# Queries loaded as pairs of tokens, and turned by products with the identity into every other column

## The chip, the cores and the metric

The kernel runs on one NeuronCore of a Trainium2 chip. The core has five engines with instruction streams of their own: TensorE (PE, matrix products; its weight loads are listed apart as PEld), VectorE (DVE), ScalarE (ACT), GpSimd (POOL) and SyncE (SP), which here only issues DMAs. Sixteen DMA engines carry all transfers. SBUF is the on-chip memory of 128 partitions; PSUM takes the results of TensorE. The metric is the device time of one execution in microseconds (us).

## The reference

Linear attention with decay (4 batches, 8 heads, 768 tokens, head dimension 64), and a mixture of 8 experts behind it, of which each token takes 2. Cut to what matters:

```python
for b in range(nb):                                    # blocks of 64 tokens
    qb, kb, vb = (q[:, :, sl], k[:, :, sl], v[:, :, sl])
    intra = np.einsum('bhic,bhjc->bhij', qb, kb) * Dmask[None]
    intra = np.einsum('bhij,bhjd->bhid', intra, vb)
    inter = np.einsum('bhid,bhde->bhie', qb * lam_pow[None], kv_state)
    out[:, :, sl] = intra + inter
    kv_state = lam_block[None, :, None, None] * kv_state + np.einsum('bhsd,bhse->bhde', kb_dec, vb)
x = out.transpose(0, 2, 1, 3).reshape(3072, 512)
# gate: logits and noise scale from x, the two best of 8 experts for each token, their softmax weights
for e in range(8):
    out2[mask] += top2_w[mask, k, None] * (np.maximum(x[mask] @ w1[e], 0.0) @ w2[e])
```

q, k and v are float32 in HBM, laid out (batch, head, token, 64): the 64 numbers of one token and one head are 256 bytes in a row, and the next token of the same head follows them directly.

## The kernel before

The attention takes the first 140 us or so, the experts the rest. The attention works in chunks of C = 128 tokens, two chunks (a = 0 and 1) to a step, and u = 0 to 11 numbers the 12 steps (NST); three steps make a batch (NW). Heads are taken in pairs (HP = 4 pairs), so that a pair's 2 x 64 numbers fill 128 partitions.

`load(u, nm)` brings a step's k, q or v to SBUF, tokens on the partitions: two transfers on SP's queue, one for each chunk, each 128 tokens x 8 heads x 64 numbers. `trans_k(u)` and `trans_q(u)` turn keys and queries, so that the 64 numbers of a head lie on the partitions and the tokens along them: for each chunk four transposes of 128 x 128 on TensorE, one for each pair of heads, into a bank of PSUM, which ACT (DVE at u = 0) copies to SBUF; for the queries DVE makes beside it qTs, the copy multiplied by the decay QS. `scores(u)` multiplies turned queries and keys, and DVE multiplies the mask in (tile `at`). `kv(u)` makes the state, `intra` and `inter` the two parts of the output (PSUM banks pO and pKV), `kdecay` the decayed keys (ACT), `evac_o` brings the output to SBUF (ACT, tile xo), `products` and `logits` multiply it with the gate's weights, `turn_x` and `store_x` bring it to the tensor x_tok in HBM (one DMA of 512 KB on SP).

The order of the work is that of the program: each engine executes its own instructions in the order in which the loop writes them. The pass t of the loop turns keys and queries of u = t + 1, issues the loads of step t + 3, and does the second half of step t; it also issues the first expert's weights (`load_w`, tile wst, 512 KB each, on SP, at the end of the passes t = 2, 4, 5, 6, 7, 8, 10, 11), and ACT and POOL split them one pass later (`split_high`, `split_low`: tiles w1h, w2h and w1l, w2l):

```python
for t in range(NST):
    u = t + 1
    if t: products(t - 1); turn_x(t - 1)
    trans_k(u);  load(t + 3, "kt")
    trans_q(u);  load(t + 3, "qt")
    kv(u);       kdecay(t + 2)
    intra(t);    load(t + 3, "vt")
    if t: store_x(t - 1)
    inter(t, 0); evac_o(t);  logits(t - 1)
    scores(u);   inter(u, 1)
    ...
```

At the end of a pass stand routing work of earlier steps, the splitting of weights and `load_w`. The tiles kt and qt have two buffers and vt has three; PSUM has four banks under the name pS, which transposes, kv and scores use in turn. SP's DMAs signal by eight semaphores in turn, and an issue waits for the DMA that used its semaphore before, so at most eight of them are under way. In the order listings such a wait reads DMAHW0_49 to DMAHW7_49, and other waits name the engine.

At the very start two small transfers on ACT's queue make the mask: powd<-pwt (L196, to HBM) and at<-powd (L211, back in another order), then Mk (L203, L204), with which DVE's first `at` products (L361) empty the banks that kv(0) needs.

Of the kernel before, what the change touches and what calls it, by code (L numbers as in the profile page):

```python
# [26 lines left out]
AF = mybir.ActivationFunctionType  # L27
# [3 lines left out]
B, H, S, D = 4, 8, 768, 64  # L31
C = 128
NC = S // C
NCH = B * NC
HP = H // 2
# [20 lines left out]
NW = NC // 2  # L56
# [31 lines left out]
def sub(ap, offset, dims):  # L88
    return bass.AP(tensor=ap.tensor, offset=ap.offset + offset, ap=dims)
# [27 lines left out]
def kernel(  # L117
# [3 lines left out]
    nc = tc.nc  # L121
# [20 lines left out]
    QT, KT, VT = {}, {}, {}  # L142

    def load(u, nm):

        if u >= NST:
            return
        b, w = divmod(u, NW)
        at = b * H * S * D + w * 2 * C * D
        store, src, n = {"qt": (QT, q, 2), "kt": (KT, k, 2), "vt": (VT, v, 3)}[nm]  # L150
        store[u] = aw.tile([128, 2, H, D], FT, name=nm, bufs=n)
        for a in range(2):
            nc.sync.dma_start(store[u][:, a], sub(src, at + a * C * D, [[D, 128], [S * D, H], [1, D]]))  # L153

# [17 lines left out]
    for nm in ("kt", "qt"):  # L172
        load(0, nm)
    jp = ac.tile([128, 128], I32, name="jp")
    nc.gpsimd.iota(jp, pattern=[[1, 128]], base=0, channel_multiplier=-1)
    identf = consts.tile([128, 128], FT, name="identf")
# [16 lines left out]
    p = psum.tile([128, H], FT, name="pL")  # L193
    nc.tensor.transpose(p, pw[:, 1:129], identf[:H, :H])
    nc.scalar.activation(pwt[:, 0, :], p, AF.Copy)
    nc.scalar.dma_start(powd.rearrange("(a m) h -> m a h", a=2), pwt)  # L196
    mrev = aw.tile([128, C, H], FT, name="at")
    load(0, "vt")
    Mk = [ac.tile([128, HP, C], FT, name=f"Mk{s}") for s in range(2)]
    kdc = pwt[:, 0, :, None]  # L200
# [5 lines left out]
    QS = ac.tile([128, HP, C], FT, name="QS")  # L206
    p = psum.tile([128, HP, C], FT, name="pL")
# [12 lines left out]
    for nm in ("kt", "qt", "vt"):  # L220
        load(1, nm)
# [77 lines left out]
    qT, qTs, kT, KD, AT, XO, XP, PO, SA, first = {}, {}, {}, {}, {}, {}, {}, {}, {}, {}  # L299
# [3 lines left out]
    def bank():  # L303
        return psum.tile([128, HP, C], FT, name="pS", bufs=4)

    def half(i):
        return slice(i * 64, (i + 1) * 64)
# [13 lines left out]
    def trans_q(u, scaled=True):  # L321

        qT[u] = aw.tile([128, HP, 2 * C], FT, name="qT", bufs=1)
        qTs[u] = aw.tile([128, HP, 2 * C], FT, name="qTs")
        for a in range(2):
            p = bank()
            for hp in range(HP):
                nc.tensor.transpose(p[:, hp, :], QT[u][:, a, 2 * hp:2 * hp + 2, :], identf)  # L328
            cs = slice(a * C, (a + 1) * C)
            if u:  # L330
                nc.scalar.activation(qT[u][:, :, cs], p, AF.Copy)
            else:
                nc.vector.tensor_copy(qT[u][:, :, cs], p)
            if scaled and (u % NW or a):
                nc.vector.tensor_mul(qTs[u][:, :, cs], p, QS)

    def kdecay(u):
        if u >= NST:
# [297 lines left out]
    load_wgn(6)  # L636
    trans_k(0)
    trans_q(0, False)
    nc.vector.tensor_mul(qTs[0][:, :, C:], qT[0][:, :, C:], QS)
    make_mask()  # L640
# [297 lines left out]
    for t in range(NST):  # L938
        u = t + 1
# [7 lines left out]
        if u < NST:  # L947
            trans_q(u)
# [49 lines left out]
    hp = ctx.enter_context(tc.tile_pool(name="hp", bufs=1, reuse_waits="tile"))  # L998
# [189 lines left out]
    with tc.For_i(0, n_over) as it:  # L1188
# [3 lines left out]
        rows = lst[bass.ds(row, OV), :]  # L1192
# [12 lines left out]
        for f in range(FB):  # L1205
            p = psum.tile([128, OV], FT, name="pS", bufs=4)
            for d in range(DB):
                for i, (a, b) in enumerate(((0, 0), (0, 1), (1, 0))):
                    nc.tensor.matmul(p, W1[a][d][:, f * 128:(f + 1) * 128], xt(b, slice(0, OV))[:, d],
                                     start=(d == 0 and i == 0), stop=(d == DB - 1 and i == 2))  # L1210
# [3 lines left out]
        p = psum.tile([OV, DM], FT, name="pO")  # L1214
        for f in range(FB):
            for i, (a, b) in enumerate(((0, 0), (0, 1), (1, 0))):
                nc.tensor.matmul(p, ht(0, a, f, slice(0, OV)), W2[b][f // 2][:, f % 2, :],
                                 start=(f == 0 and i == 0), stop=(f == FB - 1 and i == 2))
# [31 lines left out]
```

## Time and profile before

| | |
|---|---|
| median of 3 runs | 731.28 us (727.81 to 733.37) |
| the profiled execution | 724.91 us |
| its span, first to last instruction | 723.1 us |
| PE busy | 700.6 us, 97% |
| DVE, ACT, POOL busy | 358.2, 237.6, 282.8 us |
| mean granted clock of TensorE | 0.995 |
| moved by DMA | 122.50 MB, 138698 packets, of them 87658 under 512 bytes |

A row of the profile gives a line of the code, an engine, an operation and "out<-in". One product of the code in float32 stands as two matmuls in the trace, a transpose as one. The chain of waits follows, backward from the last instruction, what each piece of work waited for; in order of time its columns are start, length and what it was. "Idle" of an engine is put down to what released it.

### The profile page before, as it was taken

How to read it: one execution, taken by the hardware profiler on the slowest of the kernel's cores; microseconds unless marked ns; L12 is line 12 of the kernel's file. 1: busy time of each engine (PE TensorE's matmuls, PEld its weight loads, DVE VectorE, ACT ScalarE, POOL GpSimd, SP SyncE). 2: the span in 40 equal slices, each digit the busy share in tenths (PEclk: the TensorE clock that was granted, in tenths of full speed). 3: DMA queues.
4: the chain of work that ended last, by engine and by line, in shares of the span. 5: the costliest groups of instructions: out<-in, count | busy, mean ns of one | idle time of the engine just before them, and what ended most of it. 6: DMA issues, size and time to landing. Idle time of an engine off the chain costs nothing.

```text
span 723.1 us, 13507 instructions
## 1 busy us (share of the span) xinstructions
PE 700.6 (97%) x4910; PEld 598.6 (83%) x4910; DVE 358.2 (50%) x815; ACT 237.6 (33%) x451; POOL 282.8 (39%) x446
## 2 busy tenths in 40 slices
PE   7999998799998999999999999999999999999996
PEld 5888887698897898898889888888888898889885
DVE  6345969777325564564445344534353454335211
ACT  1667776331123422142313231323231331314100
POOL 5210446677846453623262325124322423221311
PEclk9999999999999999999999999999999999999998
DMA  9999997971508567656456645656465656540211
GB/s 199 206 242 232 238 256 206 294 226 39 118 13 282 180 168 208 212 167 187 131 203 170 183 148 180 190 166 211 135 187 160 205 174 180 160 144 19 76 44 39
DMA packets 138698, 122.50 MB, mean 169 GB/s; under 512 B 87658, under 2 KB 106474, under 8 KB 138628
## 3 DMA queue, kind: packets, MB, share of 16 engines
q1 hardware_dynamic: 124852, 84.69, 44.2%
q0 software_dynamic: 13360, 36.38, 16.2%
q8 instruction: 40, 0.66, 0.4%
q10 hardware_dynamic: 416, 0.53, 0.3%
q14 instruction: 30, 0.25, 0.1%
HBM read 87.15 MB, written 35.55 MB: 170 GB/s over the span
## 4 chain that ended last, share of the span: by engine, by line
PE 81%; issue 6%; DMA 4%; SPq 3%; POOL 2%; ACT 1%; DVE 1%; another core or an unknown queue 1%; POOLq 0%; ACTq 0%
PE pS L861 36%; PE pO L899 15%; PE pKV L899 14%; SPq L153 2%; PE pS L358 2%; PE pKV L371 2%; DMA wst<-in_moe_w_dram 2%; PE pO L371 2%; PE pO L904 2%; PE pS L328 1%; PE pS L431 1%; PE pKV L904 1%; PE pS L315 1%; POOL out_dram L918 1%
## 5 line engine op out<-in xcount | busy, mean ns | idle before, releaser
L861 PE MATMUL pS<-xtl,w1h 128*128 128x512 f32 (+3 forms) x544 | 180.7, 332 | 1.4 <-DVE xtl L826 0.9
L861 PE MATMUL pS<-xth,w1h 128*128 128x512 f32 (+3 forms) x544 | 181.0, 333 | 0.4 <-ACT xth L825 0.4
L861 PE MATMUL pS<-xth,w1l 128*128 128x512 f32 (+3 forms) x544 | 180.4, 332 | 0.0
L867 ACT ACTIVATE ht<-pS 128x512 fp32r<-128x512 f32 (+3 forms) x136 | 65.3, 483 | 220.6 <-PE pS L861 146.1
L871 DVE SCALAR_TENSOR_TENSOR ht<-pS,ht 128x256 fp32r<-128x256 f32 (+3 forms) x176 | 76.2, 453 | 111.8 <-ACT ht L867 98.9
L899 PE MATMUL pKV<-w2h,ht 128*128 128x512 f32 x384 | 123.0, 391 | 0.0
L899 PE MATMUL pO<-w2h,ht 128*128 128x512 f32 x384 | 122.7, 391 | 0.0
L861 PEld LDWEIGHTS pS<-xtl,w1h 128*128 128x128 f32 x544 | 102.8, 189 | 10.7 <-DVE xtl L826 1.2
L861 PEld LDWEIGHTS pS<-xth,w1h 128*128 128x128 f32 x544 | 102.7, 189 | 9.7 <-ACT xth L825 0.5
L918 POOL DMA_INDIRECT out_dram<-ot,rec x46 | 61.6, 1340 | 124.9 <-DVE ot L911 112.7
L861 PEld LDWEIGHTS pS<-xth,w1l 128*128 128x128 f32 x544 | 102.8, 189 | 8.7
L899 PEld LDWEIGHTS pKV<-w2h,ht 128*128 128x128 f32 x384 | 72.1, 188 | 16.2
L899 PEld LDWEIGHTS pO<-w2h,ht 128*128 128x128 f32 x384 | 72.1, 188 | 16.1
L899 PE MATMUL pKV<-w2l,ht 128*128 128x512 f32 x192 | 75.5, 393 | 0.0
L899 PE MATMUL pO<-w2l,ht 128*128 128x512 f32 x192 | 75.4, 393 | 0.0
L814 POOL DMA_INDIRECT xg<-x_tok,rec x46 | 49.7, 1080 | 58.6 <-DMA rec<-lst 42.5
L883 POOL DMA_INDIRECT pv<-out_dram,rec x46 | 47.0, 1022 | 28.2 <-issue 28.2
L624 POOL DMA_INDIRECT lst<-recs,dest x48 | 48.3, 1007 | 11.8 <-issue 10.5
L1164 POOL COPY spacer<-ht 1x1 f32<-1x1 f32 x53 | 9.4, 177 | 106.7 <-ACT ht L867 106.6
L911 DVE SCALAR_TENSOR_TENSOR ot<-pKV,rec,pv 128x512 f32<-128x512 f32 x21 | 15.8, 751 | 66.8 <-PE pKV L899 56.9
L911 DVE SCALAR_TENSOR_TENSOR ot<-pO,rec,pv 128x512 f32<-128x512 f32 x21 | 15.7, 750 | 61.5 <-PE pO L899 59.3
L847 ACT ACTIVATE xth<-xg 128x512 fp32r<-128x512 f32 (+1 forms) x39 | 22.4, 598 | 69.0 <-DMA xg<-turned 69.0
(229 smaller groups left out, 944.8 us busy)
## 6 DMA issues: line engine op xcount, KB each, us to landing
wst<-in_moe_w_dram SPq DMA_DIRECT2D x48, 512.0 KB
turned<-ot SPq DMA_DIRECT2D x36, 256.0 KB
xg<-turned SPq DMA_DIRECT2D x144, 64.0 KB
wst<-in_moe_w_dram SPq DMA_DIRECT2D x32, 256.0 KB
kt<-in_k_dram SPq DMA_DIRECT2D x24, 256.0 KB
qt<-in_q_dram SPq DMA_DIRECT2D x24, 256.0 KB
vt<-in_v_dram SPq DMA_DIRECT2D x24, 256.0 KB
x_tok<-xc SPq DMA_DIRECT2D x12, 512.0 KB
```

The lines of the kernel that those rows point to most:

```text
L371: nc.tensor.matmul(PO[u][a][half(g), hp, :], lhs, rhs, start=n == 1, stop=n == (8 if u % NW or a else 4))
L624: st = nc.gpsimd.indirect_dma_start(out=lst, out_offset=bass.IndirectOffsetOnAxis(ap=r["dest"][:, i, c:c + 1], axis=0), in_=r["rec"][:, c, ...
L814: nc.gpsimd.indirect_dma_start(out=XG[t][:size(e, t)], out_offset=None, in_=x_tok[:rows, :], in_offset=bass.IndirectOffsetOnAxis(ap=at, ax ...
L847: nc.scalar.activation(hi, p, AF.Copy)
L861: nc.tensor.matmul(p, W1[a][d][:, fs], xt(b, cs)[:, d], start=(d == 0 and i == 0), stop=(d == DB - 1 and i == 2))
L867: nc.scalar.activation(ht(e, 0, f, cs), p, AF.Relu)
L871: nc.vector.scalar_tensor_tensor(ht(e, 1, f, c), p[:, r], 0.0, ht(e, 0, f, c).bitcast(FT), op0=OP.max, op1=SUB)
L883: nc.gpsimd.indirect_dma_start(out=PV[t][:size(e, t), :], out_offset=None, in_=out, in_offset=bass.IndirectOffsetOnAxis(ap=REC[e, t][:, 0: ...
L899: nc.tensor.matmul(p, ht(e, a, f, cs), W2[b][f // 2][:, f % 2, :], start=(i == 0), stop=(i == len(terms) - 1))
L904: nc.tensor.matmul(p[:2 * n, :], HT[0][:, f, FULL:FULL + 2 * n], W2[b][f // 2][:, f % 2, :], start=(i == 0), stop=(i == 2 * FB - 1))
L911: nc.vector.scalar_tensor_tensor(o, p, w, pv, op0=MULT, op1=ADD)
L918: st = nc.gpsimd.indirect_dma_start(out=out, out_offset=bass.IndirectOffsetOnAxis(ap=REC[e, t][:, 0:1], axis=0), in_=o, in_offset=None, bo ...
```

## The change

The queries of a step come in one transfer instead of two. A partition now holds, for each head, two neighbouring tokens (2p and 2p + 1), so that a packet is 512 bytes instead of 256, and there are 1024 of them instead of 2048. The two "chunks" of the turning are then the even and the odd tokens: `a` picks the token of the pair. A head's 64 numbers of one parity are turned by an ordinary product with the identity (64 columns of weights, the identity as the moving side), and the two heads of a pair go to the two halves of the partitions: 16 products a step instead of 8 transposes. The copies write every other column (`a::2`), so that qT and qTs have the tokens in the order as before. In the first step of a batch, where only the second chunk's qTs is needed, DVE now makes it in two halves, one for each parity.

```diff
         store[u] = aw.tile([128, 2, H, D], FT, name=nm, bufs=n)
+        if nm == "qt":
+            nc.sync.dma_start(store[u].rearrange("p a h d -> p (a h d)").rearrange("p (h x) -> p h x", h=H),
+                              sub(src, at, [[2 * D, 128], [S * D, H], [1, 2 * D]]))
+            return
         for a in range(2):
             nc.sync.dma_start(store[u][:, a], sub(src, at + a * C * D, [[D, 128], [S * D, H], [1, D]]))
...
+        rows = QT[u].rearrange("p a h d -> p (a h d)").rearrange("p (h a d) -> p h a d", h=H, a=2)
         for a in range(2):
             p = bank()
             for hp in range(HP):
-                nc.tensor.transpose(p[:, hp, :], QT[u][:, a, 2 * hp:2 * hp + 2, :], identf)
-            cs = slice(a * C, (a + 1) * C)
+                for s in range(2):
+                    nc.tensor.matmul(p[half(s), hp, :], rows[:, 2 * hp + s, a, :], identf, start=True, stop=True)
             if u:
-                nc.scalar.activation(qT[u][:, :, cs], p, AF.Copy)
+                nc.scalar.activation(qT[u][:, :, a::2], p, AF.Copy)
             else:
-                nc.vector.tensor_copy(qT[u][:, :, cs], p)
-            if scaled and (u % NW or a):
-                nc.vector.tensor_mul(qTs[u][:, :, cs], p, QS)
+                nc.vector.tensor_copy(qT[u][:, :, a::2], p)
+            if scaled and u % NW:
+                nc.vector.tensor_mul(qTs[u].rearrange("p h (c i) -> p h c i", c=2)[:, :, :, a::2],
+                                     p.rearrange("p h (c i) -> p h c i", c=2),
+                                     QS[:, :, None, a::2].to_broadcast([128, HP, 2, C // 2]))
+            elif scaled:
+                nc.vector.tensor_mul(qTs[u][:, :, C + a::2], p[:, :, C // 2:], QS[:, :, a::2])
```

On PE, in the second step (u = 1), where keys and queries are turned and kv follows, there stands before:

```order
L315 MATMUL pS<-identf,kt 128x128 [waits DMAHW7_49]
L315 MATMUL pS<-identf,kt 128x128 x3
L315 MATMUL pS<-identf,kt 128x128 [waits DMAHW1_49]
L315 MATMUL pS<-identf,kt 128x128 x3
L328 MATMUL pS<-identf,qt 128x128 [waits DMAHW3_49]
L328 MATMUL pS<-identf,qt 128x128 x3
L328 MATMUL pS<-identf,qt 128x128 [waits DMAHW4_49,PE_49]
L328 MATMUL pS<-identf,qt 128x128 x3
L403 MATMUL pS<-vt,kd 64x64 [waits DMAHW5_49,Activation_49,Pool_49]
```

and in the changed kernel (its line numbers are some lines higher):

```order
L319 MATMUL pS<-identf,kt 128x128 [waits DMAHW6_49]
L319 MATMUL pS<-identf,kt 128x128 x3
L319 MATMUL pS<-identf,kt 128x128 [waits DMAHW7_49]
L319 MATMUL pS<-identf,kt 128x128 x3
L334 MATMUL pS<-identf,qt 64x128 [waits DMAHW1_49]
L334 MATMUL pS<-identf,qt 64x128 x7
L334 MATMUL pS<-identf,qt 64x128 [waits PE_49]
L334 MATMUL pS<-identf,qt 64x128 x7
L412 MATMUL pS<-vt,kd 64x64 [waits DMAHW3_49,Activation_49,Pool_49]
```

Nothing has changed places: 8 transposes have become 16 products of half the width, which wait for one transfer instead of two.

On SP, from the first loads on, there stands before:

```order
L153 DMA kt<-in_k_dram 128x8x64 x2
L153 DMA qt<-in_q_dram 128x8x64 x2
L153 DMA vt<-in_v_dram 128x8x64 x2
L153 DMA kt<-in_k_dram 128x8x64
L153 DMA kt<-in_k_dram 128x8x64 [waits DMAHW1_49]
L153 DMA qt<-in_q_dram 128x8x64 [waits DMAHW3_49]
L153 DMA qt<-in_q_dram 128x8x64 [waits DMAHW4_49]
L153 DMA vt<-in_v_dram 128x8x64 [waits DMAHW5_49]
L153 DMA vt<-in_v_dram 128x8x64 [waits DMAHW6_49]
L234 DMA wst<-in_moe_noise_dram 24x1024 [waits DMAHW7_49]
```

and in the changed kernel (L153 is now the line of the queries, L157 that of keys and values):

```order
L157 DMA kt<-in_k_dram 128x8x64 x2
L153 DMA qt<-in_q_dram 128x8x128
L157 DMA vt<-in_v_dram 128x8x64 x2
L157 DMA kt<-in_k_dram 128x8x64 x2
L153 DMA qt<-in_q_dram 128x8x128 [waits DMAHW1_49]
L157 DMA vt<-in_v_dram 128x8x64 [waits DMAHW3_49]
L157 DMA vt<-in_v_dram 128x8x64 [waits DMAHW4_49]
L238 DMA wst<-in_moe_noise_dram 24x1024 [waits DMAHW5_49]
```

The order is the same with one row fewer a step; eight transfers under way now reach somewhat further ahead. ACT, DVE and POOL execute the same operations in the same order, but for the two half products of DVE named above.

## Rows read from the trace of the kernel before

**Rows 1.** The page: busy time of TensorE, and the DMA engines' share in 40 slices.

```profile
PE 700.6 (97%) x4910; PEld 598.6 (83%) x4910; DVE 358.2 (50%) x815; ACT 237.6 (33%) x451; POOL 282.8 (39%) x446
DMA  9999997971508567656456645656465656540211
```

**Rows 2.** Stretches of the attention: busy us of each engine, granted clock, DMA share.

```profile
58.00:68.00 10.00, 10.00 (x159) 8.49 (x152) 5.15 (x11) 7.74 (x19) 0.00 (x0) 1.00 1.08 228
110.00:124.00 14.00, 12.19 (x164) 10.65 (x161) 13.10 (x34) 9.13 (x20) 8.60 (x15) 0.88 0.88 220
```

**Rows 3.** The chain of waits in order of time, 49 to 128 us.

```profile
49.48 0.87 PE pS L315 x8
...
60.24 0.87 PE pS L328 x8
...
61.73 0.22 PE pO L371 x4
...
63.48 0.25 PE pO L371
...
78.68 0.87 PE pS L315 x8
...
82.55 5.82 DMA wst<-in_moe_w_dram
...
97.51 0.83 PE pL L585 x24
...
104.39 7.46 DMA wst<-in_moe_w_dram
...
124.65 0.87 PE pS L315 x8
...
127.01 0.14 PE pL L534
...
127.50 0.37 PE pO L371 x4
```

**Rows 4.** Waits in the first 145 us: total us, times, longest us.

```profile
ACT w1h L772 <- DMA wst<-in_moe_w_dram: 8.5, 3, 4.0
...
ACT w2h L772 <- DMA wst<-in_moe_w_dram: 5.6, 2, 3.4
...
PEld pS L403 <- ACT kT L317: 1.7, 10, 0.2
...
PE pKV L371 <- ACT xo L391: 0.7, 1, 0.7
```

**Rows 5.** The DMA view of 28 to 38 us: all packets, and SP's queue.

```profile
DMA packets 7718, 1.97 MB, mean 197 GB/s; under 512 B 7716, under 2 KB 7716, under 8 KB 7716
...
q1 hardware_dynamic: 7716, 1.94, 95.6%
```

**Rows 6.** The DMA view of 128 to 133 us (2 KB packets): SP's queue.

```profile
q1 hardware_dynamic: 831, 1.64, 96.7%
```

**Rows 7.** The start in order of time: start, us, engine, line, idle before.

```profile
8.78 1.92 PE L328 MATMUL pS<-identf,qt 128*128 128x128 f32 x8
...
9.66 0.34 ACTq L211 DMA_DIRECT2D at<-powd  x1
...
15.25 2.48 DVE L361 TENSOR_TENSOR at<-pS,Mk 128x512 f32<-128x512 f32 x4
...
16.04 0.34 PE L403 MATMUL pS<-vt,kd 128*64 128x64 f32 x4 [1.79 <-issue]
```

**Rows 8.** ScalarE by form, first 140 us: busy us, mean ns, idle before.

```profile
L331 ACT ACTIVATE qT<-pS 128x512 f32<-128x512 f32 x22 | 12.3, 637 | 0.0
...
L204 ACT ACTIVATE Mk<-at 128x512 f32<-128x512 f32 x1 | 1.1, 1150 | 6.8 <-DMA at<-powd 6.8
L210 ACT ACTIVATE QS<-pL 128x512 f32<-128x512 f32 x1 | 0.6, 598 | 2.2 <-PE pL L209 2.2
L241 ACT ACTIVATE nz<-pS 128x192 f32<-128x192 f32 x1 | 0.5, 523 | 2.7 <-PE pS L240 2.7
```

## The prediction

> **What bounds the kernel now.** I read the page first. TensorE is busy 97% of the span, and the DMA engines are full only in the first sixth of it [rows 1]: that is the attention, the only part that the change touches. So the question is which of the two sets its pace. The stretches say TensorE, with an exception: from 58 to 68 us it is busy 10.00 of 10.00 us, while the DMA engines are busy all the time as well; from 110 to 124 us it is busy only 12.19 of 14, and its granted clock averages 0.88 [rows 2]. The chain of waits shows the same in order of time. From 49 to 79 us it runs through TensorE alone, with 29.20 us for three steps, from 49.48 to 78.68, or 9.73 us a step. From 78.68 to 124.65 it leaves TensorE for the first expert's weights, with 5.82 us behind one transfer and 7.46 us behind another [rows 3]. The table of waits names who stands there: ACT, which splits the weights, waited 8.5 + 5.6 us for them [rows 4], and what it does for the next step stands behind that wait on its queue (the logits' copy, the copies of the output and of the keys), with TensorE behind those.
>
> How much that costs TensorE is read from the steps. The four from 78.68 to 124.65 took 45.97 us. At 9.73 each they would take 38.93, and two bursts of the routing's products stand among them, 0.83 us and, like the 0.49 from 127.01 to 127.50, another 0.49 [rows 3]. The rest, 45.97 - 38.93 - 1.32 = **5.7 us**, is lost to late weights, the slower clock behind the longest gap included. One more wait of TensorE, 0.7 us for ACT's copy of the output [rows 4], is behind the keys of step 2 at the start.
>
> **Part 1: what TensorE pays.** It goes from 8 transposes to 16 products a step. The transposes take 0.87 us on the chain. The new products have a shape that the trace shows: 64 columns of weights, 128 moving columns, 128 rows, two neighbours on opposite halves of the partitions. `intra` does 16 of these a step, from 61.73 to 63.48: 1.75 us [rows 3]. That is +0.88 us a step, 9.7 us over the 11 steps u = 1 to 11. All of it lies on the path, since TensorE has no gap in a common step. Something comes back: the weight loads of kv wait 0.17 us a step for ACT's copy of the keys, 1.7 us in ten steps [rows 4], and a longer trans_q covers that. Weight loads run ahead of the products, so TensorE itself loses between 0 and 1.7 us there; I take 1.0. Sum: **+8.7 us** (8.0 to 9.7).
>
> Here a rule speaks against the change. The page "TensorE: Matmul & The Clock Gate" of the Trainium skill (section Terms) calls transposes four times as fast for float32 as a plain product. By it a step's 16 products, in pairs side by side, would take 3.5 us and the sum would come out some 20 us higher; the row of `intra` shows half of that, and I go by the row. What would happen if it held is the last rival below.
>
> At u = 0 the products run at the lower clock: eight transposes take some 1.75 us there (1.92 with the last one's latency [rows 7]), so the new ones would take 3.5. They are hidden by a wait: kv(0) starts at 16.04, after an idle 1.79 us, once DVE's first masked copy at 15.25 has emptied a bank, and that copy waits for the mask, whose transfer is issued at 9.66 [rows 7]. The idle time just covers 1.75 us. I take 0; if the mask came earlier the cover would be gone, and up to 1.75 us would show. Nothing is gained by an earlier mask, since TensorE then has work until about 16 us.
>
> **Part 2: what the DMA engines save.** From 28 to 38 us nearly all packets are of 256 bytes; 7716 of them kept 16 engines busy 95.6% of 10 us, 19.8 ns each [rows 5]. A 2 KB packet, from 128 to 133 us, takes 16 x 5 x 0.967 / 831 = 93 ns [rows 6]. No row shows 512 bytes: it costs at least 19.8 ns, and at most two small ones, 39.6. The line through both sizes gives 30, which I take. The queries of a step then need 1024 x 30 / 16 = 1.94 us instead of 2048 x 19.8 / 16 = 2.53, a saving of 0.6 (0 to 1.27).
>
> Set against a step: the 6144 packets of q, k and v take 7.6 us, the store of x_tok 256 x 93 / 16 = 1.5, a weight tile another 1.5. That is 9.1 without weights, below 9.73, but 10.6 with them, so that in the passes with weights transfers fall behind by 0.9 us a step, until ACT stands waiting. Afterwards it is 10.0 (9.3 to 10.6) against a step of 9.73 + 0.79 = 10.5 us, and the passes without weights leave 2 us each to catch up. The transfers no longer fall behind, even if a 512-byte packet costs twice a small one, because the step itself has become longer. So the waits for weights should go: **-5.7 us** (4 to 6.4 together with the next term). What is late next there is TensorE itself, as in a common step. The 0.7 us at step 2 go as well: two query loads stand before those keys on SP's queue, and each gets shorter.
>
> SP also issues one DMA less a step. SP is nobody's bound; what its saving gives is in the terms above. The store of x_tok and the weight loads stand behind the queries on SP's queue and move forward with it. Against it: with eight transfers under way and one of them twice as long, a full queue holds more bytes, so weights would land later if it stayed full.
>
> **Part 3: the copies.** ACT's copies of the queries, 637 ns each, now write every other column. For a step of two no row exists. With a step of eight there are two: the mask's copy takes 1150 ns where a plain one of the same size takes 598, and one of 192 elements takes 523 [rows 8]. So the price is between 0 and 0.55 us for each of 22 copies, at most 12.1 us on ACT. I take 0 on the path: ACT is busy 7.74 of 10 us [rows 2], and 1.1 us more a step fits into its idle time, which grows by the 0.8 us of Part 1. DVE's half products replace a whole one in three steps, some 0.2 us each, beside TensorE's work; DVE is busy 5.15 of 10 there.
>
> What bears on the price between these ends: the page "SBUF — State Buffer" (section on the DMA port swizzle) puts a penalty on accesses that each touch a new line of 16 bytes, so that four-byte numbers two apart would be free and eight apart would not. The rows show only the second half of this, and they agree with it; by it the C below would not happen.
>
> **Sum.** +8.7 - 5.7 - 0.7 = **+2.3 us** on the profiled execution, whose time is 724.91: 727.2. The runs shown have their median at 731.28, 6.4 above it, so the forecast on their scale is **733.6 us**. This is 0.3%; about 1% (7.3 us) is what a measurement of this kernel tells from no change.
>
> **The rivals.**
> A. TensorE's price is hidden: steps are really set by something with slack to give, and the longer turning only shortens waits of its own, as kv's shows. Then only the gains are left: 731.3 - 6.4 = 724.9. Against it stands a TensorE busy 10.00 of 10.00 us.
> B. Slower: the weights stay late. One mechanism: ACT's wait for a weight tile is set by the queue of eight transfers in front of it, which now holds more bytes, and not by the DMA engines' load. It decides if the weights still land over 6 us after their issue. Then 5.7 us are not gained: 731.3 + 8.7 - 0.7 = 739.3. For it: 7.46 us from issue to landing [rows 3]. Against it: a step then needs less of the engines than it lasts.
> C. Slower: strided copies cost double and ACT becomes the late engine, its decayed keys and output copies delayed in each step. It decides once the added 1.1 us a step exceed ACT's slack. With all 12.1 us on the path: 731.3 + 2.3 + 12.1 = 745.7.
> D. The products do not run in pairs, or cost what the rule says: 32 matmuls of 0.109 us (0.87 / 8) are 3.5 us a step, +2.63 x 11 = 28.9 instead of 9.7. With the wait for weights gone and the 1.0 for kv back: 731.3 + 28.9 - 1.0 - 6.4 = 752.8. The row of `intra` speaks against it; only the bank differs, one for all pairs instead of two.
>
> **How the numbers follow.** Forecast 75%, A 6%, B 8%, C 7%, D 4%. The forecast's own terms (8.0 to 9.7 paid, up to 1.75 more at the start, 4 to 6.4 gained) give 731.3 + 1.6 to 731.3 + 7.5, so 733 to 739; the medians before spread by 3 us to either side. A range of 727 to 741 takes in the forecast and B and leaves out most of A, and C and D. Faster by over 1% needs 724.0 or less, just past A: 4%. Slower by over 1% needs 738.6: B, C and D in most of their cases, and the forecast's upper end, less than whole B: 16%. The remaining 80% is within 1%.
>
> **What the next profile would show.** Part 1: the turning of queries at about 1.75 us on the chain, a common step at 10.5 us, all of it TensorE. Part 2: ACT's wait for weights near zero, no gap of TensorE and no fallen clock from 88 to 124 us (shifted by some 5), DMA engines less than full from step 3 on, packets under 512 bytes fewer by 24576, queries no longer among them. Part 3: ACT's copies near 640 ns, or near 1150. The forecast is wrong if a step grows by much more or less than 0.8 us, or if the chain still leaves TensorE for the weights; and if another wait, hidden now behind these, comes forward after 140 us, where the change touches nothing.

## The result, and the profile after

The changed kernel takes 737.25 us (median of four executions, 736.0 to 741.87), the kernel before on the same chip 729.54. The ratio is 1.0146, with a 95% interval of 1.0104 to 1.0188: about 11 us slower (8 to 14), where +2.3 was forecast. The two medians alone are 7.7 us apart, the lower end of that. The time lies in the range and the sign is the one forecast; the size is off by some 8 us. The ratios below leave out disturbed executions, among them one of `two_transfers` that took 1801.77 us. The profiled execution took 737.83 us, its span is 736.0 against 723.1, so the two traces differ by 12.9.

The page of the changed kernel answers to [rows 1]: TensorE's busy time grew by 12.5 us, the DMA engines are no longer full all through the first slices, and 24767 packets fewer are under 512 bytes (24576 were forecast).

```profile
PE 713.1 (97%) x5198; PEld 609.9 (83%) x5198; DVE 358.8 (49%) x818; ACT 241.1 (33%) x451; POOL 283.0 (38%) x446
...
DMA  9887998791425656756465637555555656540211
...
DMA packets 126221, 122.53 MB, mean 166 GB/s; under 512 B 62891, under 2 KB 93995, under 8 KB 126149
```

The chain of waits of the changed kernel, answering to [rows 3] (L319 turns the keys, L334 the queries; start, us, what):

```profile
21.50 3.49 PE pS L334 x32
...
54.47 0.87 PE pS L319 x8
...
65.23 0.87 PE pS L319 x8
66.10 1.90 PE pS L334 x32
...
86.29 0.87 PE pS L319 x8
...
116.41 2.47 DVE at L370 x4
118.88 1.80 DVE ga L476
...
125.75 0.69 DVE qTs L340
...
126.49 2.09 PE pS L367 x30
...
131.23 1.20 PE pS L319 x8
```

The turning of the queries has 1.90 us on the chain instead of 0.87. Three steps from 54.47 to 86.29 take 31.82 us, 10.61 each instead of 9.73. Against [rows 3] the keys of the same steps are turned 4.99 us later at 54.47 (49.48 before), 7.61 later at 86.29 (78.68) and 6.58 later at 131.23 (124.65). So three things are to be told apart: the lead of 4.99 after only three lengthened steps, where 2.6 were due; the 0.87 a step; and what was given back between 86 and 131 us, where four more steps should have added 3.5 and the difference shrank by 1.0. The rest, from 6.6 to 12.9, arises after that point, where only the last turning of queries (0.9) belongs to the change.

At 116.41 the chain leaves TensorE, not for the weights but for DVE. The stretches of the changed kernel, answering to [rows 2] (the second one moved by the lead), and ACT's longest waits in the first 145 us, answering to [rows 4]:

```profile
58.00:68.00 10.00, 10.00 (x161) 8.76 (x158) 4.02 (x8) 6.50 (x16) 1.24 (x2) 1.00 0.72 191
116.00:131.00 15.00, 14.70 (x228) 12.30 (x224) 14.26 (x38) 9.68 (x21) 8.78 (x17) 1.00 0.60 158
```

```profile
ACT xp L430 <- PE pR L428: 22.3, 10, 2.9
ACT Mk L208 <- DMA at<-powd: 8.1, 1, 8.1
ACT qT L336 <- PE pS L334: 8.0, 20, 1.3
ACT kT L321 <- PE pS L319: 4.9, 2, 4.7
```

No weight tile is waited for. From 58 to 68 us, where no weights are loaded, the DMA engines are 0.72 busy instead of 1.08; in the steps with weights they are still full (1.00 from 80 to 100 us, 1.06 from 100 to 125). DVE is busy 14.26 of 15 us in the second stretch: that is what TensorE stands behind there. The copies of the queries cost what they did, 652 ns with every other column against 637:

```profile
L336 ACT ACTIVATE qT<-pS 128x512 f32<-128x512 f32 x22 | 14.2, 652 | 8.3 <-PE pS L334 8.0 <-ACT kT L321 0.3
```

### The profile page after: what moved, and what is told of

It is laid out like the page before. It is cut to its first block, busy times and chain, and to the rows that moved or that the text cites. A ratio compares the mean times of both kernels' runs of the same rounds, so it can differ in the third digit from the quotient of the medians.

```text
span 736.0 us, 14063 instructions
## 1 busy us (share of the span) xinstructions
PE 713.1 (97%) x5198; PEld 609.9 (83%) x5198; DVE 358.8 (49%) x818; ACT 241.1 (33%) x451; POOL 283.0 (38%) x446
## 4 chain that ended last, share of the span: by engine, by line
PE 80%; issue 6%; DVE 5%; DMA 5%; POOL 2%; SPq 1%; ACT 1%; POOLq 0%; DVEq 0%; ACTq 0%
PE pS L870 34%; PE pKV L908 14%; PE pO L908 13%; PE pS L334 3%; PE pS L367 3%; PE pKV L380 2%; PE pO L380 2%; PE pO L913 1%; PE pS L440 1%; PE pS L319 1%; DMA out_dram<-ot,rec 1%; PE pKV L913 1%; DVE at L370 1%; PE pS L832 1%; POOL out_dram L927 1%
## 5 line engine op out<-in xcount | busy, mean ns | idle before, releaser
L908 PEld LDWEIGHTS pKV<-w2h,ht 128*128 128x128 f32 x384 | 72.8, 190 | 18.3 <-DVE ot L920 1.9
L920 DVE SCALAR_TENSOR_TENSOR ot<-pKV,rec,pv 128x512 f32<-128x512 f32 x21 | 15.8, 751 | 66.5 <-PE pKV L908 53.6
L920 DVE SCALAR_TENSOR_TENSOR ot<-pO,rec,pv 128x512 f32<-128x512 f32 x21 | 15.8, 750 | 61.0 <-PE pO L908 53.6
```

The lines of the kernel that those rows point to most:

```text
L908: nc.tensor.matmul(p, ht(e, a, f, cs), W2[b][f // 2][:, f % 2, :], start=(i == 0), stop=(i == len(terms) - 1))
L920: nc.vector.scalar_tensor_tensor(o, p, w, pv, op0=MULT, op1=ADD)
```

## The experiments

A ratio is always to the kernel before, executed alternately on the same chip.

### Only the products, only the load

`products_only` is the kernel before with this edit and nothing else:

```diff
-                nc.tensor.transpose(p[:, hp, :], QT[u][:, a, 2 * hp:2 * hp + 2, :], identf)
+                for s in range(2):
+                    nc.tensor.matmul(p[half(s), hp, :], QT[u][:, a, 2 * hp + s, :], identf, start=True, stop=True)
```

> The kernel before with one part of the change: the queries are loaded as before, two transfers of 256-byte packets a step, and only the turning is done by 16 half-width products a step, with plain copies behind them. Theory 1 (the product's price on TensorE is the loss, the load is the gain): the turning shows 1.90 us on the chain as in the changed kernel, 11 x 0.88 = 9.7 us more than before; the waits for the first expert's weights stay in part, since the small packets stay. Time 738 to 744, that is at or above the changed kernel's 737.3. Theory 2 (the weights come in time only because a step has become longer, the larger packets give nothing): as the changed kernel, 736 to 738, and ACT's wait for weights is gone here too. Theory 3 (the paired load or the strided copies cost the time): near the kernel before, 729 to 732.

Ratio 1.0104 (1.0032 to 1.0176), median 735.69. Its chain, and the only wait of ACT ahead of a split of weights in the first 145 us:

```profile
54.40 0.87 PE pS L315 x8
55.27 1.90 PE pS L329 x32
...
86.22 0.87 PE pS L315 x8
...
131.05 1.20 PE pS L315 x8
```

```profile
ACT w2h L773 <- issue: 2.4, 1, 2.4
```

Three steps take 31.82 us, to the hundredth what the changed kernel takes, and at 131 us the two stand 0.2 us apart. Of ACT's 14.1 us of waits for weights, with packets of 256 bytes and two transfers a step, 2.4 are left, if that wait, for which the profile names nothing, is one for weights too. By the waits that is theory 2: in this trace the weights come in time because each step has become longer, and the larger packets add at most the rest of that wait. By the time it is not quite either theory: the median is just under the 736 to 738 of theory 2 and further under the 738 to 744 of theory 1, and the profiled execution was the fastest of four.

`pairs_only` is the other half: the kernel before with the changed `load` (the five lines of the diff in `load`), and its old turning.

> The kernel before with the load of the change alone: one transfer of 512-byte packets a step, in the change's places, but turned and copied as before, as if the tile had the old layout. The heads and tokens of the queries are mixed up by that, so the output is another one; every instruction behind the load is that of the kernel before. Theory 1 (the larger packets bring the weights in time by themselves): no wait of ACT for weights, no gap of TensorE from 88 to 124 us, 729.9 - 5 = 725, within 722 to 727. Theory 2 (only the longer step brings them in time): the waits for weights stay, 8 to 14 us of ACT, time 728 to 732.

Ratio 0.9979 (0.9950 to 1.0008): 1.5 us faster, 3.6 faster to 0.6 slower. The median, 726.83, lies in the range of theory 1. But in the profiled execution, the slowest of ten (732.68), ACT's waits for weights are still there:

```profile
ACT w2h L776 <- DMA wst<-in_moe_w_dram: 5.6, 2, 3.0
...
ACT w1h L776 <- DMA wst<-in_moe_w_dram: 2.9, 2, 2.3
```

Together 8.5 us: by the waits again theory 2. They cost TensorE little: from the keys of step 7 (82.10) to those of step 11 (124.54) it takes 42.4 us, as in a second profile of before, below. Whether the faster executions have these waits is not shown. One tile of weights is issued at 105.26 and its split begins at 112.24, 7.0 us later. That is the sign of rival B ("over 6 us after their issue"), but the kernel before has it as well (104.39 to 111.87, 7.5 us), so it does not tell whether the queue in front of a tile or the load of the DMA engines makes it late.

### The transposes kept, with the paired load

`head_transposes` keeps the load and turns one head at a time by a full-width transpose. A head's 128 columns are the two tokens of a pair, so the result has one token in each half of the partitions, and four copies of 64 partitions bring them in place; DVE scales the queries from the copies.

```diff
+                nc.tensor.transpose(p[:, hp, :], flat[:, h * 2 * D:(h + 1) * 2 * D], identf)
+            for a in range(2):
+                if u:
+                    nc.scalar.activation(qT[u][half(s), :, a::2], p[half(a)], AF.Copy)
```

> The changed kernel's paired load, 512 bytes a packet, but turned by 8 full-width transposes a step, one head each: the 128 columns of a head's pair come out as two halves of the partitions, one for each token of the pair, and four ACT copies of 64 partitions instead of two of 128 put them in place, every other column. The scaled queries are made by DVE from the copies. Theory 1 (the product's price is the loss, the load is the gain): a common step is back near 9.73 us, the waits for weights are gone or small: 729.5 - 5.7 = 724, within 722 to 727. Theory 3 (the paired load costs the time): still 735 or more. Theory 4 (ACT's 1.3 us more a step do not fit: ACT was busy 7.74 of 10 us in the step with weights): the steps with weights grow, with TensorE behind ACT's copies, 728 to 736.

Ratio 1.0066 (1.0029 to 1.0103). TensorE's turning is back at 0.87, but a common step takes 10.04 us, not 9.73 (30.12 for the three from 53.83 to 83.95 in its chain). In the stretch from 30 to 90 us, 20.2% of the chain is ACT's eight operations that decay the keys, with ACT's copies of the output behind them. Theory 1 is out. The median, 735.67, fits theory 3 (735 or more) as well as theory 4; the chain speaks for theory 4, that four copies of 640 ns instead of two were too much in that order. `head_transposes_keys_later` moves the decay behind the copies of the output:

```diff
-        kdecay(t + 2)
         scatter(1)
...
         evac_o(t)
+        kdecay(t + 2)
```

> The paired load turned by 8 full-width transposes and four half copies, as in head_transposes, with one more edit: ACT's eight operations that decay the keys of the next step stand behind its copies of the output instead of ahead of them. Theory (head_transposes lost 0.4 us a step because ACT's copy of the output came late behind the longer copies of the queries): TensorE's waits for the output's copy, 3.9 us in eight steps, go, a common step is 9.73 us again, 728 to 732 against its 735.7. Rival (the half copies cost on DVE or through the banks, not by ACT's order): as head_transposes, 733 to 737.

Ratio 1.0036 (1.0000 to 1.0073). Its chain (L334 is the turning of the queries):

```profile
53.50 0.87 PE pS L319 x8
54.37 0.87 PE pS L334 x8
...
82.70 0.87 PE pS L319 x8
```

Three steps take 29.20 us, exactly those of before [rows 3]. With TensorE's price removed and the paired load kept, the loss falls from 1.46% to 0.36%: the product's price is the greater part of it, and what is left for theory 3 is at most that rest. The kernel is still not faster than before. The same move in the kernel before, `keys_later`, was the control:

> The kernel before with the same edit alone: ACT decays the keys of the next step behind its copies of the output. Theory (ACT has slack in a common step of before): no change in the common steps, 729 to 731; where ACT stood waiting for late keys or weights, up to 2 us faster. Rival (the keys' buffer is free later, so the loads behind it start later): 1 to 3 us slower.

Ratio 1.0007 (0.9981 to 1.0033): no change, as the theory had it.

### One transfer or two

`two_transfers` cuts the paired load into two transfers of four heads, in a loop over `g`:

```diff
-            nc.sync.dma_start(store[u].rearrange("p a h d -> p (a h d)").rearrange("p (h x) -> p h x", h=H),
-                              sub(src, at, [[2 * D, 128], [S * D, H], [1, 2 * D]]))
+            for g in range(2):
+                nc.sync.dma_start(store[u].rearrange("p a h d -> p (a h d)").rearrange("p (h x) -> p h x", h=H)[:, 4 * g:4 * g + 4],
+                                  sub(src, at + 4 * g * S * D, [[2 * D, 128], [S * D, 4], [1, 2 * D]]))
```

> The changed kernel with the paired load cut into two transfers of four heads a step: packets of 512 bytes as in the change, but as many transfers as before it. Theory (the size of the packets matters, the number of transfers does not): as the changed kernel, 737.3 within 1.5. Rival (one large transfer lets the loads behind it start earlier, and so brings the weights in time): ACT's wait for weights comes back by 1 to 5 us and the time is 738 to 743. Other rival (the one large transfer lands later than two small ones and delays step 0 by the 0.8 us that TensorE waited for it): 0.5 to 1 us faster.

Ratio 1.0150 (1.0049 to 1.0252), no wait for weights, the steps as in the changed kernel (31.82 us for three). The three executions compared took 736.76 to 742.63 us, one of them well above the theory's 737.3 within 1.5, but the wait of the first rival is not there. The number of transfers does not matter here, as far as an interval of 2% tells.

### The start

`warm_start` is the changed kernel with nine products of zeros in front of kv(0) instead of one:

```diff
-WARM = (10, 2, 1)
+WARM = (10, 2, 9)
```

> The changed kernel with eight more products of zeros in front of kv(0) at the start, where TensorE stood idle for 1.87 us before its clock fell at about 18.5 us. They write nothing that is read. Theory 1 (1.7 us and more of the loss is step 1 at the lower clock, where the turning took 3.56 us instead of 1.90): the granted clock stays up from 15 to 25 us, steps later start some 2.4 us earlier, time 737.3 - 2.4 = 735, within 733 to 736.5. Rival (the start is slack that the transfers set, or the steps behind absorb it): 736.5 to 738, or more if the added products delay kv(0).

Ratio 1.0140 (1.0070 to 1.0210): nothing gained, a miss of theory 1. TensorE's start in order of time:

```profile
14.59 1.64 PE L169 MATMUL pR<-idle 128*128 128x384 bf16 x9
18.40 0.34 PE L412 MATMUL pS<-vt,kd 128*64 128x64 f32 x4 [2.18 <-issue]
...
21.53 1.97 PE L319 MATMUL pS<-identf,kt 128*128 128x128 f32 x8
```

kv(0) begins at 18.40 here, not at 16.40, since the mask landed later (DVE's copy of it begins at 16.87 instead of 14.86). So the gap was 2.18 us long instead of 1.87, and the granted clock fell all the same.

That led to the mask itself, whose landing I had taken as given. DVE's copy of it in the two halves of the change, `products_only` and `pairs_only`:

```profile
14.71 0.63 DVE L203 COPY Mk<-at 128x512 f32<-128x512 f32 x1 [3.81 <-DMA at<-powd]
```

```profile
16.14 0.63 DVE L207 COPY Mk<-at 128x512 f32<-128x512 f32 x1 [5.37 <-DMA at<-powd]
```

It begins between 14.38 and 14.71 us in six profiles with the old load, and between 14.81 and 16.87 in seven of the eight with the paired load (means 14.5 and 15.8; the eighth, `head_transposes_keys_later`, has 16.79). Most of this is the transfer, 512 KB and so not as small as I had called it: 4.7 to 5.3 us from its issue to the copy with the old load, 5.3 to 6.9 with the paired one. So the paired load delays the mask, and with it kv(0), by some 1.2 us. The number of transfers alone does not explain it, since `two_transfers`, with as many as before, has 5.8. That larger packets of the queries stand between the packets of the mask would explain it, but is not shown.

### Two more profiles, without an edit

> The kernel before, unchanged, for a second profile. Theory 1 (what separates the two first profiles outside the attention's steps belongs to the execution and not to the change: the clock that fell at step 1, and the waits after 140 us): this profile has some of them too, the turning of keys at step 1 at the lower clock or waits of TensorE of 1 to 6 us after 150 us, and its time is nearer the median of 730 than the 724.9 of the first profile. Rival (they belong to the change): a profile like the first one, 725 with the clock up from 16 to 28 us.

> The changed kernel, unchanged, for a second profile. Theory 1: the steps again 0.87 us longer each, the start and the waits after 140 us different from the first profile by a few us. Rival (both belong to the change): the same 3.2 us at step 1 and the same 5 us after 140 us.

They took 724.67 and 735.51 us. The first time is the rival's, not that of theory 1. So both profiles of before are faster than its medians (729.5 and 729.1), and what its other executions lose is in no trace of it. In `after_2` three steps again take 31.82 us, and the start and the end differ from the first profile by 1.8 and 4.2 us, as theory 1 had it. In the second profile of before, the granted clock of the stretches at the start and ACT's longer wait for weights in the first 145 us (the other, on w1h, is 1.1):

```profile
16.00:20.00 4.00, 3.32 (x44) 2.81 (x45) 2.45 (x5) 0.00 (x0) 1.82 (x3) 0.59 1.31 213
20.00:24.00 4.00, 4.00 (x44) 3.67 (x44) 1.21 (x2) 2.39 (x4) 1.93 (x5) 0.55 0.89 179
```

```profile
ACT w2h L772 <- DMA wst<-in_moe_w_dram: 5.4, 2, 4.0
```

The lower clock at step 1 belongs to the execution: it is here too (the keys' turning takes 1.97 us at 19.14, against 1.09 at 18.70 in the first profile). In `gate_later`, below, which starts as the changed kernel does, the clock stays up (1.00 from 16 to 24 us, keys turned in 1.09 at 19.00). And the loss to late weights is not fixed either: ACT waited 6.5 us for them in this execution of before instead of 14.1, and the keys of step 11 were turned at 122.60 instead of 124.48, although step 2 had begun 1.6 us late. The four steps from 80.11 to there took 42.5 us, where the first profile took 46.0.

### What is late next

`early_weights` issues five of the weight loads one step earlier in the kernel before:

```diff
-LOADS = {2: [(1, 0)], 4: [(1, 1)], 5: [(1, 2)], 6: [(1, 3)], 7: [(2, 0)], 8: [(2, 1)], 10: [(2, 2)], 11: [(2, 3)]}
+LOADS = {2: [(1, 0)], 3: [(1, 1)], 4: [(1, 2)], 5: [(1, 3)], 6: [(2, 0)], 7: [(2, 1)], 10: [(2, 2)], 11: [(2, 3)]}
```

> The kernel before with five of its loads of the first expert's weights issued one step earlier and nothing else changed. Theory (late weights cost TensorE some 5.7 us): ACT's waits for weights go, TensorE has no gap from 88 to 124 us, 724 to 726. Rival (the transfer engines have no room in the earlier steps, so that keys, queries and values come late instead): the waits move to the queries and keys, 728 to 733.

Ratio 0.9985 (0.9952 to 1.0017): no change. The waits for weights are gone, and two of the waits between 86 and 125 us show what stands in their place:

```profile
ACT xc L432 <- DMA x_tok<-xc: 5.0, 1, 5.0
...
PE pS L328 <- ACT xc L432: 4.2, 1, 4.2
```

A store of x_tok, on the same queue of SP as the loads, came late instead, and TensorE stood 4.2 us behind it. That is the rival's kind of outcome, and its time (728 to 733), on a store and not on the queries.

`gate_later` takes DVE's side of the same place, in the changed kernel: seven small operations of the second group's gate are moved behind the scaled queries and masked copies of step 10.

```diff
-FILLA, FILLB, FILLC = {4: 24, 5: 24, 6: 20, 7: 20, 8: 19, 9: 19, NST - 1: 24}, 2, 4
+FILLA, FILLB, FILLC = {4: 24, 5: 24, 6: 20, 7: 20, 8: 12, 9: 26, NST - 1: 24}, 2, 4
```

> The changed kernel with seven of the small DVE operations of the second group's gate moved behind the scaled queries and the masked copies of step 10; the same operations, in another order on DVE. Theory (what is late at step 10 now that the weights are in time is DVE, whose gate work stands ahead of the scaled queries; TensorE waits for it about 0.9 us): the scaled queries of step 10 come some 2 us earlier, the wait of TensorE in front of the scores there is gone, 0.5 to 1 us in the trace, 736.5 in the timing, too little to be told from 737.3. Rival (another wait takes its place): the steps from 115 to 130 us as long as before.

Ratio 1.0192 (1.0128 to 1.0255), not faster. Its chain:

```profile
113.45 2.46 DVE at L370 x4
115.91 1.81 DVE ga L476
...
121.01 1.28 DVE qTs L340 x2
...
133.35 0.19 PE pL L543
```

The scaled queries begin 5.1 us after `ga` instead of 6.9, and TensorE's step there takes 10.75 us (keys at 116.31 and 127.06) instead of 11.90: the theory's gain is in the trace. But the routing's count (L543), which needs the end of the gate, now waits 2.9 us, until 133.35, a wait that the changed kernel does not have. From the masked copies of step 9 to that count DVE works almost without a gap, 19.9 us here; in the changed kernel the count begins at 134.72 in the timeline, 18.3 us after 116.41. So the rival was right in the end: whatever is put first, something that TensorE needs is last.

`splits_later` asks how much of this is POOL's doing, in the kernel before: the weights' low parts are made later.

```diff
-LOW = {5: [(1, 0)], 6: [(1, 1)], 7: [(1, 2)], 8: [(1, 3)], 9: [(2, 0)], 10: [(2, 1)]}
+LOW = {5: [(1, 0)], 6: [(1, 1)], 7: [(1, 2)], 10: [(1, 3), (2, 0), (2, 1)]}
```

> The kernel before with two of POOL's splits of weights, 2.35 us each, moved from the steps in which DVE works through the second group's gate to the last step that has splits; nothing else changed. Theory (from the masked copies of step 9 to the routing counts of the second group DVE works without a gap, 18.9 us in the first profile of before, and that, not the weights alone, sets the time there; single operations of 0.22 us take 1.6 to 2.4 us beside POOL's split): the first of them falls back to 0.22 us, the stretch of DVE to 16 or 17 us, and the kernel becomes 1 to 2 us faster than before, 0.997 to 0.999 of it. Rival (the late weights set the time there by themselves): DVE's stretch is shorter but TensorE's gaps are as long, ratio 1.000; or the splits come too late for the first expert, ratio above 1.002 with a wait at the first products of the experts.

Ratio 1.0063 (1.0032 to 1.0094): slower. DVE's timeline, and one wait of TensorE from 86 to 160 us:

```profile
110.49 0.22 DVE L467 SCALAR_TENSOR_TENSOR ga<-zc 128x64 f32<-128x64 f32 x1
...
117.42 1.29 DVE L335 TENSOR_TENSOR qTs<-pS,QS 128x512 f32<-128x512 f32 x2 [2.43 <-ACT qT L331]
...
136.14 5.70 DVE L566 TENSOR_SCALAR past<-past,base 128x8 f32<-128x8 f32 x1
```

```profile
PE pL L449 <- DVE pos L568: 5.8, 1, 5.8
```

`ga` is back at 0.22 us, but the scaled queries begin at 117.42, as late as ever: now DVE waits 2.43 us for ACT, which stood 5.9 us behind a weight tile. That is longer than in either profile of before (3.4 and 1.3 at this tile); whether the edit did it is not shown. So in these traces the late weights and DVE's queue each set the time at this place, and to take one away gained nothing. And the splits, now three in a row, met another operation of DVE, L566, which takes 0.23 us for another group (at 94.06 in this profile); it took 5.70, until the last of them ended, with TensorE 5.8 behind it.

## Why the prediction was right and wrong

**Part 1, the price of the products: right.** `intra`'s row gave 1.75 us for sixteen; the chain shows 1.90 for the turning, 0.14 less for the kv behind it, and the step has grown by 0.87 to 0.88 us. No gap covered any of it, so rival A falls. The rule quoted from the Trainium skill ("TensorE: Matmul & The Clock Gate", Terms) would have made it 3.5, and D with it; the measurement decides, 1.90 against 0.87 is a factor of 2.2 for products of half the width in pairs side by side. Here the trace does not agree with four.

**The 1.0 us back from kv: wrong, it was 0.** The wait is gone where it stood, but the same total stands one place earlier, in front of the turning of the queries:

```profile
PEld pS L334 <- ACT xc L441: 1.7, 10, 0.2
```

By the starts in the timeline it costs TensorE about 0.1 us a step in either place: before, it went on from the eight transposes of the keys after 0.88 us and from those of the queries, to kv, after 0.96; now it goes on from those of the keys after 0.97. So nothing came back.

**u = 0 and step 1, taken as 0: off by 2.4 us in the profiled execution.** I costed the step before kv(0) and found the cover just wide enough. That held: the products took 3.47 us there, and kv(0) begins at 16.40 instead of 16.04. I did not cost step 1 at the lower clock. In this execution the granted clock was 0.74 and 0.50 from 16 to 24 us (0.50 is the lower of its two levels), after an idle 1.87 us in front of kv(0); in the first profile of before it stayed at 1.00 after an idle 1.79:

```profile
16.00:20.00 4.00, 2.69 (x42) 2.25 (x43) 2.84 (x6) 0.02 (x1) 1.43 (x2) 0.74 1.31 199
20.00:24.00 4.00, 4.00 (x32) 3.67 (x32) 0.00 (x0) 1.75 (x3) 2.32 (x6) 0.50 1.03 231
```

At that clock the keys and the queries of step 1 took 1.90 + 3.49 us on the chain instead of 0.87 + 1.90. But it comes and goes with the execution: with the changed start the first 27 us cost between 0.6 less and 4.1 us more than the term says (`gate_later`, `after_2`), and with the old start 0 to 1.9 more than the first profile of before. Below that lies a part that belongs to the change: the mask, for which kv(0) waits, lands some 1.2 us later with the paired load (0.4 in this execution). I had costed the cover as if its end were fixed. For the medians the term is worth perhaps 1 to 2 us, an estimate from these leads.

**Part 2, the step that failed.** That the waits for weights go was right. That the DMA engines are less than full was right only in steps without weights; with them they are as full as they were, and the kernel with the small packets, `products_only`, has the lower share there. Of the changed kernel and of `products_only`:

```profile
100.00:125.00 25.00, 25.00 (x450) 22.31 (x448) 18.39 (x50) 18.60 (x44) 13.30 (x19) 1.00 1.06 254
```

```profile
100.00:125.00 25.00, 25.00 (x448) 22.31 (x444) 17.95 (x50) 18.18 (x44) 13.34 (x19) 1.00 0.94 222
```

"So the waits for weights should go: -5.7 us" was not right, in its size and in its cause.

- Size: between the keys of steps 7 and 11 the change gave back 3.5 + 1.0 = 4.5 us against the first profile of before (5.7 forecast there). The second profile of before gives back 3.5 of these without any change, 1.6 + 1.9; so do `keys_later` and `pairs_only`, with 42.1 and 42.4 us for the four steps. Of a gain read from one execution, about 1 is the change's. The 0.7 at step 2 is the same: the wait is gone in the changed kernel, and in the second profile of before too.
- Cause: not the packets, as far as single traces show it. The longer step alone brings the weights in time (`products_only`), the packets alone do not (`pairs_only`). What a 512-byte packet costs stays open. From 28 to 38 us, with 19.8 ns for each of the 4504 small packets, the 1191 others come out at 22 ns; from 60 to 80 us, with 93 ns for each of the 640 of 2 KB, at 37. These are estimates from the rows below, and the 30 taken lies between them.

```profile
DMA packets 5696, 1.76 MB, mean 176 GB/s; under 512 B 4504, under 2 KB 5695, under 8 KB 5695
...
q1 hardware_dynamic: 5695, 1.74, 72.2%
```

```profile
DMA packets 9770, 4.39 MB, mean 220 GB/s; under 512 B 7562, under 2 KB 9127, under 8 KB 9767
...
q1 hardware_dynamic: 9767, 4.35, 83.7%
```

- What is late next: I named TensorE itself. In the changed kernel it is DVE, and its row stood in [rows 2]: 13.10 of 14 us busy, beside TensorE's 12.19. I gave all of TensorE's missing time to the weights, because the chain went through them. `early_weights`, `gate_later` and `splits_later` each took one of the things away and found the next within a few us: a store behind the same queue, the gate's end, DVE's wait for ACT.

**Part 3, the copies: right.** 652 ns against 637, within the bounds of 0 to 0.55 us at their lower end, and nothing on the path. C falls. The rule on lines of 16 bytes that the forecast took from the page "SBUF — State Buffer" of the Trainium skill (section on the DMA port swizzle) agrees with this row for a step of two.

**B**, weights late by the queue in front of them, did not come in the changed kernel. Its sign, a tile over 6 us late, is in `pairs_only` (7.0 us) and in the kernel before (7.5) alike; its mechanism is not shown.

**The sum again.** Paid 9.7 instead of 8.7; the start 1 to 2 in the medians; gained 1 to 4.5 instead of 6.4. That gives +6 to +11, against the measured 11 (8 to 14). The two halves measured alone, 7.6 (2.3 to 12.8) for the products and -1.5 (-3.6 to 0.6) for the load, add up to about 6, with intervals that reach 11. That the time fell into the range has some luck in it: the forecast was put on a median before of 731.28, which four executions then put at 729.54; 11 us above the 731.28 would have been just outside.

**What stays open** is the time after the attention. In the first trace some 5 us of the 12.9 arise there. From the start of the keys' turning of step 11 to the end of the span takes 598.6, 600.3, 600.5, 600.3 and 599.6 us in `before`'s two profiles, `keys_later`, `early_weights` and `products_only`. `splits_later` has 604.5 with a wait of 5.8 of its own. It takes 600.6 to 608.9 in the eight profiles with the paired load (604.8 in the first of the changed kernel, 600.6 in the second). The waits that make it up differ; the largest is one scatter of the experts' output in the chain of `two_transfers`:

```profile
290.42 9.96 DMA out_dram<-ot,rec
```

That would look like a cost of the paired load, but the timings do not bear it out: in `pairs_only`, `head_transposes` and `head_transposes_keys_later` the profiled execution was the slowest of ten, and `pairs_only` is not slower than before in the median. The forecast named such a wait as a thing that could upset it. No run settles why it is seen in profiles with this load.

## What to carry to other kernels

A gap that the chain of waits puts down to one engine is worth only what the next-latest one leaves: read the busy time of every engine in that stretch before counting the gap as a gain, and read it in a second execution. When one edit both lengthens the bounding engine's step and lightens the transfers, the lengthening alone may end the wait for the transfers; then the lighter transfers have nothing left to give. Two half-width products with the identity, side by side, cost here 2.2 times a full-width transpose in float32, so a layout that saves packets but forces this is paid for on TensorE in every step.

## What the runs showed of the hardware

- A small operation of DVE can last as long as the split of POOL beside it: `ga`, 0.22 us by itself, took 1.80 in the chain of the changed kernel beside a split of 2.35 us, and another, 0.23 us by itself, took 5.70 beside three splits in a row; each ended when the split did. The page "SBUF — State Buffer" of the Trainium skill (Practical consequences, under its table of engine ports) says that an operation of DVE with two operands in SBUF contends with one of GpSimd that reads SBUF. The trace agrees: `ga` reads two operands from SBUF and so does the split, while DVE's masked copies (L370), with one operand in PSUM, kept their 2.48 us for four where a split ran beside some of them.
- ACT's copies of 64 partitions, half of them from one half of PSUM's partitions into the other half of SBUF's, every other column, took 640 ns for 512 columns (`head_transposes`, mean of 44), as long as on 128 partitions without the move (652).
- A packet of 512 bytes came out at 22 and at 37 ns in two stretches, against 19.8 for one of 256 (the estimates above).
- The mask, a transfer of 512 KB issued by ACT, took 4.7 to 5.3 us with the queries' packets of 256 bytes on SP's queue beside it, and 5.3 to 6.9 with packets of 512 bytes.
- Between two executions of the kernel before, the granted clock of step 1 (1.00 and 0.55 from 20 to 24 us) moved TensorE's steps by 1.6 us, and the waits for weights (14.1 and 6.5 us of ACT) by 3.5; the whole change was forecast at 2.3.
